# A chain of attention, mixer and routed experts: the turned keys' transposes behind the values' products, two conversion parts a step sooner, free banks first in the banks' turn

## The chip, the cores and the metric

One Trainium2 chip, one of its cores. The metric is the device time of one execution in microseconds (us). The kernel before takes 421.62 us, the median of 3 runs (421.58 to 422.22). The measurement of this kernel tells changes of some 0.2% from none.

## The reference

Three stages follow one another; each takes the output of the one before. Cut to what matters:

```python
# 1 attention with a decaying state: 2 batches, 8 heads, 768 tokens, 48 wide
y[:, :, t] = einsum('bhd,bhde->bhe', r_t, state + einsum('bhd,bhe->bhde', u * k_t, v_t))
state = w * state + einsum('bhd,bhe->bhde', k_t, v_t)
# 2 token mixing, then channel mixing, x is [2, 768, 384]
u = x + (relu(x^T @ w_tok1) @ w_tok2)^T      # 768 -> 256 -> 768
x = u + relu(u @ w_ch1) @ w_ch2              # 384 -> 1536 -> 384
# 3 eight experts; a token takes the expert of its largest logit, or,
#   where its local gate is 0.5 or more, that of the token before it
out = p[e] * (relu(x @ w1[e]) @ w2[e])       # 384 -> 1024 -> 384
```

## The kernel before, in words

**Attention** goes in 12 chunks of 128 tokens, t = 0 to 11, six for each batch. The loop over t is a pipeline written out by hand: each engine's instructions stand in the order in which the loop calls its helpers, and nothing reorders them. One turn of the loop works on several chunks at once. It calls, in this order: `old(t+1)` (PE starts the tile kp, L447), `scores(t+1)` (16 PE products into two tiles at0 and at1, L406), `pre_rk(t+2)` (DVE scales the keys and queries of a chunk, tile rk, L372), `pre_ks(t+2)` (four PE transposes of rk into the tile kt, L383, and a copy by ACT to ks, L385), `conv_ahead` (ACT, L315), `masks(t+1)` (DVE, am, L418), `beta(t+1)` (PE, into kp, L455), `pre_beta(t+2)` (DVE, pp, L377), `update(t+1)` (PE adds keys times values into kp, L464), `state(t+1)` (ACT L476, or DVE L480), `values(t)` (PE products into the tile y, L431 with the old state and L436 with the masked scores), `pre_bonus2(t+1)` (ACT copies beta out of kp, L391, and makes eight pieces of bon, L394), some parts of a weight conversion, `finish(t)` (DVE adds y and bon to x, L485; ACT and POOL split x into xh, L489, and xl, L490), from t = 7 a piece of token mixing `mix2`, then `turn(t-1)` (three PE transposes of x into the tile tp, L500, copied to xT by ACT, L501) and, from t = 4, `mix1` (PE, L357 to L359).

`pre_ks` makes ks two chunks ahead: update(t+2), in the next turn of the loop, is its only reader. It is called for all chunks but the last of each batch (5 and 11); in the loop that is at t = 0, 1, 2, 4, 5, 6, 7 and 8.

**PSUM banks.** Five banks are given out in rotation: `ps_tile` takes the next number of `turn_of` = [0, 1, 2, 3, 4], by a counter `nps`. A new tile can be written once the tile that had its bank, five calls earlier, has been read. In the loop kp, at0, at1, kt, y and tp go through this rotation; the accumulators of the mixing (`acc_tile`) have banks of their own.

**Weight conversion.** The mixer's weights arrive as 64-bit words (tile raw) in 16 blocks. Each is turned into two fp32r tiles, high and low: ACT takes the magnitude (L315), DVE works on it in three parts (L323 with L324; L328; L330), and `conv_finish` casts the high half (ACT, L291) and subtracts for the low half (POOL, L292). `conv_do(n)` works off n parts; conv_finish of a block comes at the start of the next block's first part. During attention the numbers of parts a turn are in `CONV_N`; later they are entries of a list `later`.

**Channel mixing** is a list of steps (n, f), n the quarter of the tokens, f = 0 to 11 the twelfth of the hidden width. `chan_step` makes nine PE products into a tile c of the bank rotation (`ch1`, L357 to L359), splits the result (ACT hh L362, DVE hl L363), queues `ch2`, nine products into three accumulators, which is called two steps later, and takes one entry off `later`. For n = 0 the accumulators lie in banks 2, 3 and 4 of the rotation, which then runs over banks 0 and 1 alone; after the last product of n = 0 DVE adds the three accumulators to xT (L676), and the rotation runs over all five banks again. The experts' stage behind it is not touched by the change.

Of the kernel before, what the change touches and what calls it, by code (L numbers as in the profile page):

```python
# [22 lines left out]
NCH = S // 128  # L23
NT = B * NCH
# [6 lines left out]
WARM = (6, 12, 3)  # L31
T1 = 4
CONV_N = (0, 2, 2, 3, 2, 3, 2, 2, 2, 2, 1, 0)
CONV_B = (0, 1, 0, 0, 0, 1, 1, -1, 0, 0)
HI_MIN, HI_MAX = (float(x) for x in np.array([0x38100000, 0x47EFFFFF], np.int32).view(np.float32))

# [39 lines left out]
def _emit(ctx, tc, a_in, wu, u_row, wt1, wt2, wc1, wc2, wgl, wex, cst_in, cst_a, out):  # L76
# [37 lines left out]
    turn_of, nps = [0, 1, 2, 3, 4], [0]  # L114

    def ps_tile(name, shape=(128, 512), k=None):
        if k is None:
            k = turn_of[nps[0] % len(turn_of)]
            nps[0] += 1
        return psw.tile(list(shape), F32, tag=f"w{k}", name=name)  # L120
# [10 lines left out]
    def CA(name):  # L131
        a, b = CSTA[name]
        return cta[:, a:b]
# [4 lines left out]
    def load_a(t, part=None):  # L138
        if t not in a_t:
            rk = ap.tile([128, 1024], F32, tag="rk", name=f"rk{t}", bufs=4)  # L140
            v = ap.tile([128, DM], F32, tag="v", name=f"v{t}", bufs=4)
            a_t[t] = (rk, v)
        for p, (dst, c0) in enumerate(zip(a_t[t], (0, 1536))):
            if part is None or p == part:
                nc.sync.dma_start(out=dst, in_=a_in[t, :, c0:c0 + dst.shape[1]])
# [15 lines left out]
    def warm_up(n):  # L161
        for _ in range(n):
            nc.tensor.matmul(warm_ps, lhsT=warm[:, 0:128], rhs=warm[:, 0:384], start=True, stop=True)
# [103 lines left out]
    def conv_load():  # L267
        n = nload[0]
        if n >= len(conv) or (n >= 10 and not cpool_):
            return  # L270
        nload[0] += 1
        k, h = conv[n]
        src = wt1 if k == 0 else wt2 if k == 1 else None
        if src is None:
            src = (wc1, wc2)[k % 2][(k - 2) // 2]
        if n < 10:
            raw = rawp.tile([128, 768, 2], I32, tag="raw", name="raw")
        else:
            raw = cpool_[0].tile([128, 768, 2], I32, tag=f"e{n - 10}", name="raw")
        src = src.bitcast(I32)  # L280
        if k > 1 and k % 2 == 0:
            src = src.rearrange("p (c n) -> p c n", c=3)[:, :, h * 512:(h + 1) * 512]
            nc.sync.dma_start(out=raw.rearrange("p (c n) t -> p c (n t)", c=3), in_=src)
        else:
            nc.sync.dma_start(out=raw.rearrange("p n t -> p (n t)"), in_=src[:, h * 1536:(h + 1) * 1536])
        conv_raw.append(raw)
# [52 lines left out]
    def conv_ahead():  # L339
        if abs_next[0] < 8:  # L340
            conv_abs(abs_next[0])
            abs_next[0] = 8
# [9 lines left out]
    def conv_do(n=3):  # L352
        for _ in range(n):
            next(conv_work, None)
# [15 lines left out]
    def pre_rk(t):  # L370
        rk = a_t[t][0]
        nc.vector.tensor_tensor(out=rk, in0=rk, in1=PP.rearrange("p a q j -> p (a q j)"), op=ALU.mult)  # L372
# [6 lines left out]
    def pre_ks(t):  # L379
        rk = a_t[t][0]  # L380
        kt = ps_tile("kt")
        for q in range(4):
            nc.tensor.transpose(kt[:, q * 128:(q + 1) * 128], rk[:, 512 + q * 128:512 + (q + 1) * 128], CA("ident"))  # L383
        ks_t[t] = ap.tile([128, 512], F32, tag="ks", name="ks")
        nc.scalar.copy(ks_t[t], kt)  # L385
# [3 lines left out]
    def pre_bonus2(t):  # L389
        beta = ap.tile([128, 8], F32, tag="beta", name="beta")  # L390
        (nc.scalar.copy if t % NCH else nc.vector.tensor_copy)(beta, beta_t.pop(t))  # L391
        bon = ap.tile([128, 8, D], F32, tag="bon", name="bon")
        for h in range(8):
            nc.scalar.activation(out=bon[:, h], in_=heads(a_t[t][1])[:, h], func=ACTF.Copy, scale=beta[:, h:h + 1])  # L394
        bon_t[t] = bon
# [4 lines left out]
    def scores(t):  # L400
        rk = a_t[t][0]
        at_t[t] = [ps_tile("at0"), ps_tile("at1")]
        for q in range(4):
            for g in range(2):
                r0 = 64 * g
                nc.tensor.matmul(  # L406
                    at_t[t][g][:, q * 128:(q + 1) * 128],
                    lhsT=rk[r0:r0 + 64, 512 + q * 128:512 + (q + 1) * 128],
                    rhs=rk[r0:r0 + 64, q * 128:(q + 1) * 128],
                    start=True,  # L410
                    stop=True,
                )

    def masks(t):
        am_t[t] = []
        for g, at in enumerate(at_t.pop(t)):
            am = ap.tile([128, 4, 128], F32, tag=f"am{g}", name=f"am{g}")
            nc.vector.tensor_tensor(  # L418
                out=am, in0=at.rearrange("p (h j) -> p h j", h=4), in1=C("strict").unsqueeze(1).to_broadcast([128, 4, 128]), op=ALU.mult
            )  # L420
            am_t[t].append(am)
# [20 lines left out]
    def old(t):  # L442
        kp = ps_tile("kp")
        kp_t[t] = kp[:, 0:384].rearrange("p (q e) -> p q e", q=4)
        beta_t[t] = kp[:, 384:392]
        if t % NCH in range(1, NCH - 1):
            nc.tensor.matmul(kp_t[t], lhsT=CA("ident"), rhs=sts[(t - 1) % 3], start=True, stop=False)  # L447

    def beta(t):
        pp = pp_t.pop(t)  # L450
        alone = t % NCH in (0, NCH - 1)
        for q in range(4):
            for a in range(2):
                r = slice(64 * a, 64 * a + 64)
                nc.tensor.matmul(  # L455
                    beta_t[t][r, 2 * q:2 * q + 2], lhsT=pp[:, q * 128 + 64 * a:q * 128 + 64 * a + 64], rhs=uw[:, q], start=alone, stop=alone
                )
# [118 lines left out]
    for t in range(NT):  # L576
        if t + 3 < NT:
            load_a(t + 3, 0)
        if t == 0:
            conv_load()  # L580
            conv_load()
        grow = t + 1 < NT and (t + 1) % NCH < NCH - 1
        if t + 1 < NT:
            old(t + 1)
            scores(t + 1)
            if t == 0:
                warm_up(WARM[2])
        if t + 2 < NT:
            pre_rk(t + 2)
            if (t + 2) % NCH < NCH - 1:  # L590
                pre_ks(t + 2)
        conv_ahead()
        if t + 1 < NT:
            masks(t + 1)
            beta(t + 1)
        if t + 2 < NT:
            pre_beta(t + 2)
        if grow:
            update(t + 1)
            state(t + 1)  # L600
        values(t)
        if t + 1 < NT:
            pre_bonus2(t + 1)
        if t + 3 < NT:
            load_a(t + 3, 1)
        if t < NT - 1:
            conv_do(CONV_N[t])
        finish(t)
        if t == 0:
            conv_abs(0)  # L610
        if t == NT - 1:
            conv_do(CONV_N[t])
        if t >= 7:
            mix2(*m2.pop(0))
        if t == 10:
            usplit(0)
        if t >= 1:
            turn(t - 1)
            m1.append(t - 1)
            if t >= T1:  # L620
                for _ in range(2):
                    if m1:
                        mix1(m1.pop(0))
# [39 lines left out]
    def ch2(n, f, h):  # L663
        b, half = divmod(n, 2)
        ch, cl = W[f"c2{f // 4}"]
        if f == 0:
            if n == 0:
                turn_of[:] = [0, 1]
            ch_acc[n] = [acc_tile(c) if n else ps_tile("acc", (128, 384), 2 + c) for c in range(3)]
        acc = ch_acc[n]  # L670
        for c in range(3):
            o = (f % 4) * 384 + c * 128
            mm3(acc[c], ch[:, o:o + 128], cl[:, o:o + 128], *h, f == 0, f == 11)
            if f == 11:
                u = xT[b][:, c, half * 384:(half + 1) * 384]
                nc.vector.tensor_tensor(out=u, in0=u, in1=acc[c], op=ALU.add)  # L676
        if n == 0 and f == 11:
            turn_of[:] = [0, 1, 2, 3, 4]

    later = []  # L680

# [19 lines left out]

    conv_tail(CONV_B[0])
    turn(11)
    chan_step(0, 0)
    conv_tail(CONV_B[1])
    mix1(11)
    conv_tail(CONV_B[2])
    chan_step(0, 1)
    chan_step(0, 2)
    conv_tail(CONV_B[3])  # L710
    for half in range(2):
        for c in range(3):
            mix2(1, half, c, -1 if half else (2, 0, 1)[c])
            conv_tail(CONV_B[4 + 3 * half + c])
    actx.close()
# [503 lines left out]
        for _ in side:  # L1219
            pass  # L1220

    later.extend([lambda j=j: conv_do(2 - j % 2) for j in range(16)])
    later.append(conv_do)
    order = [(0, 3), (1, 0), (1, 1), (1, 2)]
    for f in range(4, 8):
        order += [(0, f), (1, f - 1)]
# [163 lines left out]
```

## Time and profile before

| what | us |
|---|---|
| median of 3 runs | 421.62 (421.58 to 422.22) |
| the profiled execution | 421.5 |
| its span, first to last instruction | 420.0 |
| PE busy (matmul) | 397.4, 95% of the span |
| DVE busy | 274.7, 65% |
| ACT busy | 192.1, 46% |
| POOL busy | 88.4, 21% |
| mean granted TensorE clock | 0.987 of full speed |

The profiled execution lies 0.12 us under the median, and 1.5 us of it lie outside the span. Of the three stages, attention with token mixing takes about the first 100 us, channel mixing and routing go to about 200 us, and the experts take the rest. PE is busy in nearly all of the span, so the profile is read by the 22.6 us in which PE is idle: in which stretch they lie, what PE waited for there, and what the engine it waited for had been doing. In timelines each row is a run of equal instructions: its start, its length, engine and line, operation, tiles, and in brackets the idle time of that engine just before it with what ended it. Start to start, equal matmuls show the pace at which PE takes them.

### The profile page before, as it was taken

What the parts mean: (1) busy time and instruction counts of PE and PEld (TensorE: products, weight loads), DVE (VectorE), ACT (ScalarE), POOL (GpSimd) and SP (SyncE); (2) the same over time, 40 slices, a digit from 0 to 9 for tenths busy, and PEclk for the clock granted to TensorE, in tenths of its full rate; (3) what the DMA queues carried; (4) which work ended last, traced back from release to release, by engine and by line L of the source; (5) the groups of instructions that cost most, each with busy time, mean ns of one, the idle gap of its engine ahead of it and who ended that gap; (6) DMA issues with size and microseconds to landing.
All of it is one profiled execution on the core that took longest, in us unless ns stands there. A gap on an engine that the chain in (4) does not pass through costs nothing. (4 is left out here: it accounts for less than half of the span.)

```text
span 420.0 us, 8633 instructions
## 1 busy us (share of the span) xinstructions
PE 397.4 (95%) x3348; PEld 378.8 (90%) x3348; DVE 274.7 (65%) x592; ACT 192.1 (46%) x459; POOL 88.4 (21%) x83
## 2 busy tenths in 40 slices
PE   7896987999999998999999999999999999999994
PEld 3685967899999998899999999999999999999994
DVE  6799877775678987447433256759777677675430
ACT  1786566484144333221312121643755665654531
POOL 2016143333122331100000002033241222122110
PEclk9999998999999999999999999999999999999998
DMA  7746462303194000010100013781789867562000
GB/s 259 276 119 224 164 214 90 132 29 108 19 368 159 2 1 0 2 56 2 56 2 1 2 57 104 290 299 28 291 283 419 268 211 247 198 197 89 20 23 14
DMA packets 18336, 55.88 MB, mean 133 GB/s; under 512 B 3921, under 2 KB 7795, under 8 KB 18290
## 3 DMA queue, kind: packets, MB, share of 16 engines
q1 hardware_dynamic: 16370, 49.96, 33.8%
q0 software_dynamic: 1920, 5.32, 4.1%
q8 instruction: 27, 0.44, 0.4%
q14 instruction: 19, 0.16, 0.1%
HBM read 52.31 MB, written 5.91 MB: 139 GB/s over the span
## 5 line engine op out<-in xcount | busy, mean ns | idle before, releaser
L362 ACT ACTIVATE hh<-c 128x384 fp32r<-128x384 f32 x48 | 23.6, 492 | 89.7 <-PE c L359 76.8
L1038 DVE TENSOR_TENSOR we<-wr,we 128x768 fp32r<-128x768 f32 x54 | 51.6, 960 | 15.0 <-ACT we L1037 15.0
L363 DVE SCALAR_TENSOR_TENSOR hl<-c,hh 128x384 fp32r<-128x384 f32 x48 | 26.5, 553 | 40.9 <-ACT hh L362 40.9
L362 ACT ACTIVATE hh<-e 128x256 fp32r<-128x256 f32 (+1 forms) x72 | 25.2, 350 | 57.7 <-PE e L359 45.1
L363 DVE SCALAR_TENSOR_TENSOR hl<-e,hh 128x256 fp32r<-128x256 f32 (+1 forms) x72 | 27.3, 379 | 35.7 <-ACT hh L362 35.6
L357 PE MATMUL acc<-hh,c 128*128 128x384 f32 x144 | 49.6, 344 | 0.0
L358 PE MATMUL acc<-hh,c 128*128 128x384 f32 x144 | 48.4, 336 | 0.2 <-POOL c L292 0.2
L359 PE MATMUL acc<-hl,c 128*128 128x384 f32 x144 | 48.2, 335 | 0.0
L1037 ACT CAST we<-wr 128x768 fp32r<-128x768 f32 x56 | 46.0, 829 | 3.0 <-DMA wr<-in_wex 3.0
L357 PE MATMUL acc<-we,hh 128*128 128x384 f32 x120 | 42.8, 357 | 0.0
L358 PE MATMUL acc<-we,hl 128*128 128x384 f32 x120 | 40.4, 337 | 0.0
L359 PE MATMUL acc<-we,hh 128*128 128x384 f32 x120 | 40.4, 336 | 0.0
L358 PE MATMUL c<-uh,c 128*128 128x384 f32 x108 | 36.3, 336 | 2.1 <-POOL c L292 2.1
L292 POOL TENSOR_TENSOR c<-f,c 128x768 fp32r<-128x768 f32 x12 | 23.0, 1915 | 65.9 <-ACT c L291 65.9
L357 PE MATMUL c<-uh,c 128*128 128x384 f32 x108 | 36.2, 336 | 0.0
L359 PE MATMUL c<-ul,c 128*128 128x384 f32 x108 | 36.1, 335 | 0.0
L358 PEld LDWEIGHTS acc<-hh,c 128*128 128x128 f32 x144 | 27.1, 188 | 0.5 <-POOL c L292 0.5
L357 PE MATMUL e<-gx,we 128*128 128x256 f32 x96 | 27.2, 284 | 0.0
L359 PEld LDWEIGHTS acc<-hl,c 128*128 128x128 f32 x144 | 27.0, 188 | 0.0
L357 PEld LDWEIGHTS acc<-hh,c 128*128 128x128 f32 x144 | 27.0, 188 | 0.0
L359 PE MATMUL e<-gx,we 128*128 128x256 f32 x96 | 27.0, 281 | 0.0
L358 PE MATMUL e<-gx,we 128*128 128x256 f32 x96 | 27.0, 281 | 0.0
(243 smaller groups left out, 977.8 us busy)
## 6 DMA issues: line engine op xcount, KB each, us to landing
wr<-in_wex SPq DMA_DIRECT2D x32, 768.0 KB
raw<-in_wc SPq DMA_DIRECT2D x12, 768.0 KB
rk<-in_a_in SPq DMA_DIRECT2D x12, 512.0 KB
raw<-in_wt SPq DMA_DIRECT2D x4, 768.0 KB
v<-in_a_in SPq DMA_DIRECT2D x12, 192.0 KB
x<-yscr ACTq DMA_DIRECT2D x12, 192.0 KB
xs<-rows SPq DMA_DIRECT2D x8, 192.0 KB
xs<-row SPq DMA_DIRECT2D x4, 192.0 KB
```

The costliest lines, as they stand in the source:

```text
L292: nc.gpsimd.tensor_tensor(out=ls, in0=f, in1=hs.bitcast(F32), op=ALU.subtract)
L357: nc.tensor.matmul(ps, lhsT=lh, rhs=rh, start=first, stop=False)
L358: nc.tensor.matmul(ps, lhsT=ll, rhs=rh, start=False, stop=False)
L359: nc.tensor.matmul(ps, lhsT=lh, rhs=rl, start=False, stop=last)
L362: nc.scalar.activation(out=hi, in_=ps, func=ACTF.Relu)
L363: nc.vector.scalar_tensor_tensor(out=lo, in0=ps, scalar=0.0, in1=hi.bitcast(F32), op0=ALU.max, op1=ALU.subtract)
L1037: nc.scalar.copy(hi[:, cs], raw[:, cs])
L1038: eng.tensor_tensor(out=lo[:, cs], in0=raw[:, cs], in1=hi[:, cs].bitcast(F32), op=ALU.subtract)
```

## The change

`pre_ks(t+2)` is called behind `values(t)` and `pre_bonus2(t+1)`, no longer right behind `pre_rk(t+2)`. The entries of `later` follow a table `CONV_C`, in which the ninth to twelfth entry are all of two parts. After the last step of n = 0 the rotation starts anew with the two banks 0 and 1, the one whose turn it was first, and then goes to 2, 3 and 4.

```diff
+CONV_C = (2, 1, 2, 1, 2, 1, 2, 1, 2, 2, 2, 2, 1, 2, 1, 1)
...
         if t + 2 < NT:
             pre_rk(t + 2)
-            if (t + 2) % NCH < NCH - 1:
-                pre_ks(t + 2)
         conv_ahead()
...
         values(t)
         if t + 1 < NT:
             pre_bonus2(t + 1)
+        if t + 2 < NT and (t + 2) % NCH < NCH - 1:
+            pre_ks(t + 2)
...
         if n == 0 and f == 11:
-            turn_of[:] = [0, 1, 2, 3, 4]
+            a = nps[0] % 2
+            turn_of[:] = [a, 1 - a, 2, 3, 4]
+            nps[0] = 0
...
-    later.extend([lambda j=j: conv_do(2 - j % 2) for j in range(16)])
-    later.append(conv_do)
+    later.extend([lambda j=j: conv_do(j) for j in CONV_C])
```

The table adds a line, so that the lines of the changed kernel have numbers one higher. On PE only the eight groups of transposes move. Here is the turn t = 4 on PE, before (rk_648 is the chunk 6, am_668 belongs to chunk 4):

```order
L406 MATMUL at_756<-rk_541 128x128
L383 MATMUL kt<-cta,rk_648 128x128 x4
L455 MATMUL kp<-uw,pp 64x2 x8
L431 MATMUL y<-st_186,rk_439 64x96 x8
L436 MATMUL y<-v_440,am_668 64x48 x2
```

and with the change, down to the transposes of x that follow:

```order
L407 MATMUL at_756<-rk_541 128x128
L456 MATMUL kp<-uw,pp 64x2 x8
L432 MATMUL y<-st_186,rk_439 64x96 x8
L437 MATMUL y<-v_440,am_668 64x48 x2
L437 MATMUL y<-v_440,am_670 64x48 x2
L384 MATMUL kt<-cta,rk_648 128x128 x4
L501 MATMUL tp<-cta,x 128x128 x3
```

The transposes of chunk 6 stood between the scores of chunk 5 and everything else of the turn; now the products of beta and y pass them. On ACT, in the same turn, before:

```order
L501 COPY xT_535<-tp 128x3x128
L385 COPY ks<-kt 128x512
L315 ACTIVATE f<-raw 128x768
L391 COPY beta<-kp 128x8
L394 ACTIVATE bon<-v_542,beta 128x48 x8
```

and with the change:

```order
L502 COPY xT_535<-tp 128x3x128
L316 ACTIVATE f<-raw 128x768
L392 COPY beta<-kp 128x8
L395 ACTIVATE bon<-v_542,beta 128x48 x8
L386 COPY ks<-kt 128x512
```

The copy to ks moved behind the eight pieces of bon. Since kt and y change places in the bank rotation, their neighbours' banks change too: the tile at1 of a turn takes the bank of y of the turn before the last, not that of a kt. In the channel mixing the casts of the last four blocks stand one step earlier on ACT; the third of them (into c_1997) before:

```order
L362 ACTIVATE hh<-c_2136 128x384
L315 ACTIVATE f<-raw 128x768
L362 ACTIVATE hh<-c_2161 128x384
L291 CAST c_1997<-f 128x768
L362 ACTIVATE hh<-c_2189 128x384
L547 CAST uh<-xT_1202 128x384 x3
```

and with the change:

```order
L363 ACTIVATE hh<-c_2113 128x384
L316 ACTIVATE f<-raw 128x768
L363 ACTIVATE hh<-c_2138 128x384
L292 CAST c_1997<-f 128x768
L363 ACTIVATE hh<-c_2166 128x384
L363 ACTIVATE hh<-c_2190 128x384
L292 CAST c_2052<-f 128x768
L548 CAST uh<-xT_1202 128x384 x3
```

Each hh belongs to one channel step. The cast into c_1997 stood one hh ahead of the casts of uh; now it stands two ahead of them, and the fourth cast, which stood behind uh, stands in front of it. The order of instructions on POOL and SP is the same in both kernels.

## Rows read from the trace of the kernel before

**Rows 1.** Windows: stretch, length, busy us of each engine (instructions), granted clock, DMA share.

```profile
20.00:40.00 20.00, 15.79 (x318) 13.47 (x317) 19.13 (x26) 16.92 (x54) 7.04 (x5) 1.00 0.44 141
...
200.00:420.00 220.00, 213.38 (x1478) 210.68 (x1477) 125.05 (x331) 96.41 (x203) 37.25 (x38) 0.99 0.43 148
```

**Rows 2.** Waits of PE: line, waited for, us in total, times, longest.

```profile
PE kt L383 <- DVE rk L372: 7.8, 4, 4.0
PE c L358 <- POOL c L292: 2.1, 2, 1.6
...
PE acc L358 <- POOL c L292: 0.2, 1, 0.2
```

**Rows 3.** Timeline of PE, turns t = 4 and 5.

```profile
39.74 0.63 PE L383 MATMUL kt<-cta,rk 128*128 128x128 f32 x4 [3.95 <-DVE rk L372]
...
44.08 0.55 PE L500 MATMUL tp<-cta,x 128*128 128x128 f32 x3
...
46.64 1.16 PE L406 MATMUL at<-rk 64*128 64x128 f32 x16
```

**Rows 4.** Timeline of DVE, turns t = 3 to 7.

```profile
37.91 0.55 DVE L485 TENSOR_TENSOR x<-y,bon 128x384 f32<-128x384 f32 x1
38.38 1.22 DVE L372 TENSOR_TENSOR rk<-rk,PP 128x1024 f32<-128x1024 f32 x1
...
47.83 1.29 DVE L418 TENSOR_TENSOR am<-at,cst 128x512 f32<-128x512 f32 x2 [1.73 <-PE at L406]
...
54.09 2.39 DVE L372 TENSOR_TENSOR rk<-rk,PP 128x1024 f32<-128x1024 f32 x1
...
63.57 1.02 DVE L363 SCALAR_TENSOR_TENSOR t1l<-acc,t1h 128x384 fp32r<-128x384 f32 x2 [2.21 <-ACT t1h L362]
64.51 1.78 DVE L372 TENSOR_TENSOR rk<-rk,PP 128x1024 f32<-128x1024 f32 x1
```

**Rows 5.** Timeline of ACT, turn t = 4.

```profile
41.75 0.92 ACT L315 ACTIVATE f<-raw 128x768 f32<-128x768 f32 x1 [0.76 <-DMA raw<-in_wt]
42.57 0.14 ACT L391 COPY beta<-kp 128x8 f32<-128x8 f32 x1
```

**Rows 6.** Timeline of PE, turns t = 6 to 8.

```profile
56.63 0.63 PE L383 MATMUL kt<-cta,rk 128*128 128x128 f32 x4 [1.28 <-DVE rk L372]
...
59.74 0.55 PE L500 MATMUL tp<-cta,x 128*128 128x128 f32 x3 [0.49 <-ACT beta L391]
...
66.44 0.63 PE L383 MATMUL kt<-cta,rk 128*128 128x128 f32 x4 [2.32 <-DVE rk L372]
...
71.20 0.44 PE L357 MATMUL acc<-t,t1h 128*128 128x384 f32 x1
...
75.56 0.65 PE L383 MATMUL kt<-cta,rk 128*128 128x128 f32 x4
...
78.81 0.44 PE L357 MATMUL acc<-t,t1h 128*128 128x384 f32 x1
```

**Rows 7.** Windows, two stretches of lower granted clock (columns as in rows 1).

```profile
40.50:44.00 3.50, 3.50 (x64) 3.50 (x60) 3.46 (x4) 2.71 (x9) 2.19 (x2) 0.51 0.56 219
...
67.80:71.30 3.50, 3.50 (x61) 3.41 (x57) 2.19 (x4) 3.47 (x14) 0.00 (x0) 0.51 0.21 63
```

**Rows 8.** Timeline of PE in the channel mixing.

```profile
161.57 0.34 PE L359 MATMUL acc<-hl,c 128*128 128x384 f32 x1
161.74 0.40 PE L357 MATMUL c<-uh,c 128*128 128x384 f32 x1
163.69 0.44 PE L358 MATMUL c<-uh,c 128*128 128x384 f32 x1 [1.55 <-POOL c L292]
...
176.43 0.34 PE L359 MATMUL acc<-hl,c 128*128 128x384 f32 x1
177.35 0.44 PE L357 MATMUL c<-ue,c 128*128 128x384 f32 x1 [0.58 <-DVE xT L676]
```

**Rows 9.** Timeline of POOL, turn t = 4.

```profile
38.40 2.88 POOL L292 TENSOR_TENSOR t<-f,t 128x768 fp32r<-128x768 f32 x1 [3.27 <-ACT t L291]
```

## The prediction

> **What bounds the kernel now.** I read the windows first. PE is busy in 213.4 of the last 220 us, and in only 15.8 of the stretch from 20 to 40 us, where DVE is busy in 19.1 of 20 [rows 1]. So the kernel is bound by PE, except in the attention turns t = 2 to 7, where DVE hands work to PE late. The list of PE's waits says which: the largest entry is kt on rk, 7.8 us in four waits, then 2.1 us on POOL's low halves, and 0.2 more of that kind [rows 2]. The timelines give the single waits: 3.95 us at t = 4 [rows 3], 1.28 at t = 6 and 2.32 at t = 7 [rows 6]; these three make 7.55 of the 7.8. The reader should see what stands behind each on PE: beta, the state's and the values' products need nothing of that rk, yet wait with kt, since an engine works in order.
>
> **The change, part by part.** The sum is made against the profiled execution, 421.5 us, 0.12 under the median of the runs.
>
> *The transposes, t = 4.* Nothing is added or removed; eight groups of four transposes and eight copies change place. Without kt in front, PE's next obstacle is the bank of y(4), which is now that of y(3), read by x. That ends at 37.91 + 0.55 = 38.46 [rows 4]. rk ends at 38.38 + 1.22 = 39.60, so kt, behind y, no longer waits. Then tp(3) takes the bank of kp(5), as it did before; its reader is the copy of beta, which ends at 42.57 + 0.14 = 42.71, since it stands on ACT behind L315, which waits for the DMA of raw [rows 5]. That end doesn't move: the copy to ks, which leaves its place ahead of L315, lay in ACT's idle time. So tp(3) starts at about 42.75, not at 44.08 [rows 3]: **-1.33**. Of the 3.95 us only a third comes back, and the wait for the DMA is what is late next.
>
> *t = 5 and 6.* The scores at 46.64 [rows 3] come 1.33 sooner. DVE waited 1.73 us for them; its rk ended 1.73 before 47.83, at 46.10, and the scores' new time, 46.50, is still behind that, so DVE gains the full 1.33 [rows 4]. From there it works without a gap to the rk that ends at 54.09 + 2.39 = 56.48, now 55.15. On PE the scores of chunk 7 ended at 56.63 - 1.28 = 55.35, now 54.02. From kt to tp there are 59.74 - 0.49 - 56.63 = 2.62 us of work [rows 6]. With kt last of it, kt runs at about 56.1, behind rk's end at 55.15. So the wait of 1.28 goes. The 0.49 us behind it were for a copy of beta that stood on ACT behind the copy to ks; ks now comes after it. Both together: **-1.77**, and tp(5) starts at 56.64.
>
> *t = 7.* Everything is now 3.10 sooner: t1l and the rk that follows it on DVE [rows 4] end at 64.51 + 1.78 - 3.10 = 63.19. The scores ended at 66.44 - 2.32 = 64.12, now 61.02. Ahead of kt now come beta, update and y. At t = 8, where PE doesn't wait, kt, beta, update and y take 78.81 - 75.56 = 3.25 us [rows 6]; 0.6 of it is kt, so kt is reached at 63.7, half a us behind rk. **-2.32**.
>
> *The clock.* From kt to mix2 the turn t = 7 takes 71.20 - 66.44 = 4.76 us, t = 8 takes 3.25 for the same instructions [rows 6]: 1.51 us go to a granted clock of 0.51, the 1.2 GHz level, from 67.8 to 71.3 us, and the same is seen from 40.5 to 44.0 [rows 7]. Each time PE had just stood still for 2.3 to 4 us. With the wait of t = 7 gone I take the clock to stay at 2.4 GHz there: **-1.51**. At t = 4 I count nothing for the clock, since the wait for beta's copy sets the end there.
>
> *New bank waits.* at1 now takes the bank of the y before, so half of the scores wait for x(t-1) on DVE. At t = 6 the scores begin at 52.9 and x ends at 53.62 - 1.33 + 0.55 = 52.84: just level. The trace of before shows no such wait; the nearest row is a bank wait of 0.49 [rows 6]. From below: nothing, when x is always earlier. From above: 0.49 in each of the eight turns, 3.9 us. I take one, **+0.5**, since only t = 6 stands so close; at t = 2 and 3 such waits are swallowed by the 3.95 us of t = 4. The moved copies cost nothing: ks is read only by update in the next turn, behind sixteen score products; without that cover a copy's 0.6 us would be paid. From t = 8 on DVE isn't late, so the gain stays.
>
> Attention in sum: -1.33 - 1.77 - 2.32 - 1.51 + 0.5 = **-6.4**.
>
> *Conversion.* The last four blocks are finished one channel step sooner. A step is 18 products at 0.17 us start to start [rows 8], 3.1 us. The product at 163.69 came 1.95 us after its forerunner instead of 0.17, a loss of 1.78; the block would now be there 3.1 sooner, 1.3 before it is wanted. The last block's 0.2 [rows 2] goes too. **-2.0.** What could spoil it: four steps running carry two parts each, eight instead of six, and DVE falls behind; bounds are 0 and 2.0, and I take the full one since a late part must lose over 1.3 us to matter. DVE's own hl, queued behind the parts, is read two steps later, which covers it. The third wait of this kind, the rest of the 2.1, lies ahead of the blocks that move and stays.
>
> *Banks.* At 177.35 a product waits for DVE's last addition over a bank; 177.35 - 176.43 - 0.17 = 0.75 is lost [rows 8]. With banks 0 and 1 first it has a free one. **-0.75**; below that nothing, above nothing more.
>
> After this PE is the bound to the end, and the loads follow its pace. 421.5 - 6.4 - 2.0 - 0.75 = **412.3 us**. Its own range is 411.0 (no new waits, the fourth kt wait of 0.25 and further small ones gone) to 413.3 (two more waits of 0.49).
>
> **The rivals.**
>
> *The clock stays low.* At t = 4 two waits of about 2 us remain, with short work between, and if PE's pauses still pull the clock down there or at t = 7, the 1.51 us come once more: 413.8. For it: both low stretches follow pauses [rows 3, 6 and 7]. Against it: at t = 7 no pause of a size is left. Beside this stands the Trainium skill, "TensorE: Matmul & The Clock Gate", Part 4: PE-mode transpose, which says that transposes don't count as PE being busy as other matmuls do; by it kt wouldn't help to keep the clock up, and the time would be this rival's. No row here shows transposes alone.
>
> *POOL gets ahead of rk.* At t = 4 rk began at 38.38, and POOL's subtraction, which took 2.88 us, at 38.40 [rows 4, 9]. Had POOL been first, rk would take as at 54.09, 2.39 instead of 1.22, and all of DVE would be 1.17 later: 413.5. The Trainium skill, "SBUF — State Buffer", SBUF: two separate sides, has this as a lock on a port pair that DVE and POOL share, held for a whole instruction by whoever comes first; the 2.39 against 1.22 agrees.
>
> *The wait only changes its name.* If x is late at t = 6 and 7, at1 waits where kt did, and 1.28 + 2.32 = 3.6 us stay: 415.9. For it: DVE is nearly full from 20 to 40 us. Against: x stands ahead of rk on DVE, so the new wait ends 1.2 us before the old one would.
>
> *The two later edits give nothing*, should DVE's backlog hold up the blocks and another wait stand behind the bank's: 412.3 + 2.75 = 415.1.
>
> *Slower.* The bank of at1 closes a ring: y on PE, x on DVE, scores on PE, masks on DVE. Before, scores ran beside x. If x ends last in every turn, each of the eight turns grows by up to 0.49, and the kt waits are all handed on to at1; nothing of the 6.4 is left, and 421.5 + 3.9 - 2.75 = 422.7. It decides once half the scores take longer than the rk of 1.22 us that DVE works on meanwhile; all the scores take 1.16 [rows 3], so it is unlikely.
>
> *No effect.* DVE sets the pace so fully that every wait ends when it did, whatever PE does in between: 421.5. Against it: DVE itself waits for PE's scores, 1.73 us [rows 4].
>
> **How the numbers follow.** Chances: forecast 0.55, clock 0.14, POOL first 0.08, wait renamed 0.10, later edits nothing 0.06, slower 0.04, unchanged 0.03. The range from 410.0 to 415.3 holds the first three and the fifth, with 1 us below the forecast's own range for a second clock stretch gone; it leaves out 0.17. A measurement of this kernel tells 0.2%, 0.84 us, from no change: faster 0.93, same 0.03, slower 0.04.
>
> **What would show it.** Right: no wait of kt on rk over 0.5 us; at t = 4 a wait of y for x and one of tp for beta, some 2 us each; a clock near 1.00 from 60 to 80 us; the first product of channel mixing some 6.4 us sooner; of the waits on POOL's low halves only the one near 100 us; none of L357 on L676. Wrong: at or y waiting over 1 us at t = 6 and 7, low clock at t = 7, or a low half still awaited at the last blocks.

## The result

The changed kernel takes 412.23 us, the median of 4 runs (411.33 to 412.77), against 421.92 (421.58 to 422.63) for the kernel before on the same chip. The ratio is 0.9766, with a 95% interval of 0.9743 to 0.9789: 9.7 us faster, where 9.2 (412.3 us) was forecast. The profiled execution took 412.36 us, its span 410.7; before it was 420.0, so the traces differ by 9.3.

**The profile after.** First PE's list of waits (line and what it waited for, us in total, times, longest). Line numbers are one higher than before; the rows left out stand in both kernels:

```profile
PE y L432 <- DVE x L486: 2.0, 1, 2.0
...
PE c L359 <- POOL c L293: 0.6, 1, 0.6
PE tp L501 <- ACT beta L392: 0.4, 1, 0.4
PE at L407 <- DVE x L486: 0.3, 1, 0.3
```

Of the entries of [rows 2], kt on rk is gone with all its 7.8 us, the 2.1 us on POOL have become the one wait of 0.6 that was said to stay, and the 0.2 is gone; no wait on DVE's last addition (now L677) is left. New are y on x, 2.0, and at on x, 0.3. The 0.4 of tp on beta is not the old 0.49 of t = 6 but a wait at t = 8. The forecast had also named a wait of tp for beta at t = 4, of some 2 us: this trace has none.

The timeline of PE shows where the time came from. The turn t = 4, answering to [rows 3]:

```profile
35.51 0.63 PE L456 MATMUL kp<-uw,pp 128*64 128x2 f32 x16
38.13 1.55 PE L432 MATMUL y<-st,rk 128*64 128x96 f32 x16 [1.98 <-DVE x L486]
39.46 1.89 PE L437 MATMUL y<-v,am 128*64 128x48 f32 x32
41.29 1.12 PE L384 MATMUL kt<-cta,rk 128*128 128x128 f32 x4
42.20 0.85 PE L501 MATMUL tp<-cta,x 128*128 128x128 f32 x3
...
45.62 1.16 PE L407 MATMUL at<-rk 64*128 64x128 f32 x16
```

and the turns t = 6 to 8, answering to [rows 6]:

```profile
56.79 0.49 PE L501 MATMUL tp<-cta,x 128*128 128x128 f32 x3
...
63.82 0.63 PE L384 MATMUL kt<-cta,rk 128*128 128x128 f32 x4
64.20 0.42 PE L358 MATMUL acc<-t,t1h 128*128 128x384 f32 x1
...
67.46 1.64 PE L407 MATMUL at<-rk 64*128 64x128 f32 x16
...
73.84 0.55 PE L501 MATMUL tp<-cta,x 128*128 128x128 f32 x3 [0.43 <-ACT beta L392]
```

The reader should see that kt runs without a wait in both; that y, kt and tp of t = 4 take nearly double their usual time (e8 below shows it: 0.88, 1.09, 0.66 and 0.55 us); and that the scores at 67.46 take 1.64 us instead of 1.16. The clock, in two stretches (columns as in [rows 1]), after:

```profile
36.00:48.00 12.00, 10.02 (x129) 9.40 (x127) 10.83 (x14) 7.08 (x22) 5.52 (x3) 0.72 0.54 187
62.00:76.00 14.00, 13.57 (x196) 11.70 (x191) 13.87 (x20) 9.82 (x33) 4.36 (x3) 1.00 0.40 124
```

and before:

```profile
36.00:48.00 12.00, 8.26 (x101) 7.70 (x102) 10.20 (x13) 7.57 (x24) 5.54 (x3) 0.86 0.53 176
62.00:76.00 14.00, 11.68 (x142) 9.98 (x140) 9.94 (x13) 7.83 (x23) 6.53 (x4) 0.88 0.32 109
```

The granted clock at t = 7 is now 1.00 and was 0.88; at t = 4 it is 0.72 and was 0.86. The second low stretch went, the first grew longer.

**Time by stage.** Each mark is the start of a group of instructions in a PE timeline: the scores of chunk 5 and of chunk 6 (at), the first product of the channel mixing (c), the first transpose of the routing (tr), the end of the span. The experiments stand here too, so that each can be read by stage:

| kernel | to scores 5 | to scores 6 | to first c | to first tr | to the end | span |
|---|---|---|---|---|---|---|
| before | 34.6 | 12.0 | 53.3 | 79.1 | 241.0 | 420.0 |
| after | 34.4 | 11.2 | 48.2 | 75.9 | 241.0 | 410.7 |
| e1 transposes | 36.5 | 10.2 | 47.9 | 79.1 | 241.0 | 414.7 |
| e2 conversion | 34.6 | 14.1 | 54.7 | 76.7 | 243.0 | 423.2 |
| e3 banks first | 34.6 | 13.5 | 54.6 | 78.2 | 241.2 | 422.2 |
| e4 pairs only | 34.8 | 13.1 | 53.3 | 79.1 | 241.0 | 421.3 |
| e5 change again | 36.4 | 10.9 | 48.1 | 75.9 | 243.0 | 414.2 |
| e6 old pairs | 37.1 | 9.8 | 48.3 | 75.9 | 241.2 | 412.2 |
| e7 late abs | 35.0 | 9.0 | 48.7 | 75.9 | 242.9 | 411.4 |
| e8 fill t4 | 34.4 | 10.2 | 48.1 | 75.9 | 242.8 | 411.5 |
| e9 fill before | 34.6 | 10.7 | 51.8 | 79.1 | 242.9 | 419.1 |
| e10 ks ahead | 36.6 | 13.7 | 49.7 | 75.9 | 242.9 | 418.8 |
| e11 fill, late abs | 34.4 | 8.4 | 49.6 | 75.9 | 240.9 | 409.3 |

Of the 9.3 us between the two traces, 0.2 lie before the scores of chunk 5, 0.8 at t = 4, 5.05 from there to the first c, 3.2 in the channel mixing, and none behind it. The experiments ran on two chips, e1 to e4 on one and e5 to e11 on the other, on which the kernel before takes 423.5 to 424.3 us in the median and its single executions differ by up to 6 us (421.2 to 427.1), so times there are told with intervals, of 0.3 to 0.4% to either side and not the 0.2% given at the start, and the small effects are read from the stages. The channel mixing serves best for that: from the first c to tr it takes 79.08 to 79.14 us in the four traces without the two later edits (before, e1, e4, e9) and 75.89 to 75.92 in the seven with both.

### The profile page after: what moved, and what is told of

Its sections match the earlier page's. It is cut to its first block, busy times and chain, and to the rows that moved or that the text cites. A ratio compares the mean times of both kernels' runs of the same rounds, so it can differ in the third digit from the quotient of the medians.

```text
span 410.7 us, 8643 instructions
## 1 busy us (share of the span) xinstructions
PE 396.5 (97%) x3348; PEld 379.5 (92%) x3348; DVE 274.4 (67%) x592; ACT 192.1 (47%) x459; POOL 87.3 (21%) x83
## 5 line engine op out<-in xcount | busy, mean ns | idle before, releaser
L358 PE MATMUL acc<-hh,c 128*128 128x384 f32 x144 | 49.6, 344 | 0.0
L359 PE MATMUL acc<-hh,c 128*128 128x384 f32 x144 | 48.3, 336 | 0.0
L360 PE MATMUL acc<-hl,c 128*128 128x384 f32 x144 | 48.2, 335 | 0.0
```

Of the source, the lines that this page charges most:

```text
L358: nc.tensor.matmul(ps, lhsT=lh, rhs=rh, start=first, stop=False)
L359: nc.tensor.matmul(ps, lhsT=ll, rhs=rh, start=False, stop=False)
L360: nc.tensor.matmul(ps, lhsT=lh, rhs=rl, start=False, stop=last)
```

## The experiments

**The three parts, each alone.** The kernel before with one part of the change.

e1, the transposes:

```diff
             pre_rk(t + 2)
-            if (t + 2) % NCH < NCH - 1:
-                pre_ks(t + 2)
...
-            pre_bonus2(t + 1)
+            pre_bonus2(t + 1); (pre_ks(t + 2) if t + 2 < NT and (t + 2) % NCH < NCH - 1 else None)
```

> Only the transposes (and the copies to ks) moved. Theory (each part acts where it stands, the parts add up): the part of the gain up to the first product of the channel mixing, 99.91 - 93.84 = 6.1 us in the two traces, so about 415.6 against 421.7; the waits of L358 on POOL near 160 us and of L357 on L676 near 170 us stand as before. Rival (part of the later gains is a consequence of the earlier start): more than 7 us. Rival (PSUM banks): see the run in which only the banks change places.

Measured: 416.43 us, ratio 0.983 (0.9792 to 0.9869), 7.1 us faster. Its waits, from the list of PE:

```profile
PE c L358 <- POOL c L292: 2.1, 2, 1.6
PE y L431 <- DVE x L485: 2.0, 1, 2.0
...
PE c L357 <- DVE xT L676: 0.6, 1, 0.6
```

The kt waits are gone, the later two stand untouched, and the channel mixing takes 79.1 us as before. So the parts act where they stand. The time, by its interval 5.5 to 8.8 us faster, holds the theory's 6.1 and the rival's 7 alike; the untouched channel mixing decides against the rival.

e2, the conversion's table, and e3, the banks' turn:

```diff
-    later.extend([lambda j=j: conv_do(2 - j % 2) for j in range(16)])
-    later.append(conv_do)
+    later.extend([lambda j=j: conv_do(j) for j in CONV_C])
```

> Only the table of conversion parts. Theory: 1.8 + 0.3 us of waits on POOL's low halves at the last blocks go, start to start, and some 0.1 us after each for a restart: about -2.2, 419.5. The kt waits of the attention stay at 7.8 us. Rival (DVE falls behind in the four steps of two parts and holds up something else): under 1 us of gain, with a wait of PE on hl or hh that before does not have.

```diff
-            turn_of[:] = [0, 1, 2, 3, 4]
+            a = nps[0] % 2; turn_of[:] = [a, 1 - a, 2, 3, 4]; nps[0] = 0
```

> Only the order in which the five banks are taken after the last step of n = 0. Theory: the wait of L357 on L676 goes, 0.75 us and some 0.1 for the restart: about -0.85, 420.85. Rival (another tile inherits the wait a few products later): within 0.2 us of before, with a wait of a later c or tr on L676.

Measured: e2 422.47 us, ratio 0.9947 (0.991 to 0.9984); e3 423.64, ratio 0.9998 (0.9963 to 1.0033). e2 is some 2.2 us faster, as expected, with 0.7 to 3.8 by its interval; e3's time alone can't be told from before. The stages are sharper than the times: from the first c to tr, before 79.11 us, e2 76.73, e3 78.24, after 75.90. So the table gives 2.38 and the banks 0.87, and the sum, 3.25, is what the whole change gives there, 3.21. Waits of e2:

```profile
PE kt L383 <- DVE rk L372: 7.8, 4, 4.0
...
PE acc L358 <- DVE hl L363: 1.0, 1, 1.0
...
PE c L358 <- POOL c L292: 0.6, 1, 0.6
```

The wait on hl looks like the rival's sign, but lies at 315 us, in the experts' stage; the last section comes back to it. In e3's trace no wait of L357 on L676 is left, and no later c or tr waits in its place.

**The pairing of the banks.** e4 keeps the order of before and gives y its bank ahead of kt, as the change does:

```diff
+    y_a = {}
...
-        y = ps_tile("y", (128, DM))
+        y = y_a.pop(t) if t in y_a else ps_tile("y", (128, DM))
...
             if (t + 2) % NCH < NCH - 1:
+                y_a[t] = ps_tile("y", (128, DM))
                 pre_ks(t + 2)
```

> The order of before, but kt and y get their banks in the order of the change (y first, then kt), so that only the pairing of the banks is new. Theory (what counts is what stands behind kt on PE): kt waits for rk as before, 7 to 8 us in all, and at1 now can wait for x too: between 421.5 and 422.5. Rival (the new pairing of banks brings the gain): about 415.6, with the kt waits gone.

Measured: 423.9 us, ratio 1.0018 (0.9987 to 1.0049). The row at t = 4 is the old one:

```profile
39.91 1.09 PE L383 MATMUL kt<-cta,rk 128*128 128x128 f32 x4 [3.96 <-DVE rk L372]
```

In all kt waits 6.6 us for rk, in three waits, a little under the 7 to 8 expected. So the pairing brings nothing. e6 is the counterpart: the order of the change, with kt's bank taken where it was taken before. The two calls ahead of the loop are treated alike.

```diff
-        kt = ps_tile("kt")
+        kt = kt_t.pop(t)
...
             pre_rk(t + 2)
+            if (t + 2) % NCH < NCH - 1:
+                kt_t[t + 2] = ps_tile("kt")
```

> The change, but kt and y keep the banks of before (kt's is taken first although it is used after y). Theory (the order on PE brings the gain; the new pairing only adds waits): y(4) no longer waits 2.0 us for x(3), kt(6) waits instead some 1.3 us for rk, tp(3) still waits for the copy of beta, so t = 4 ends as with the change; the scores' waits for x at t = 6 to 8 (0.2, 0.1 and 0.5 us) go. 0 to 0.8 us faster than the change, first product of the channel mixing at 93.1 to 93.9. Rival (the new pairing is needed): over 1 us slower than the change.

> The changed kernel itself, for times and rows on the chip and in the hour of the next three. Theory: a low clock of some length at t = 4, 1.00 from 60 to 80 us, 75.9 us from the first product of the channel mixing to the first tr, 241.0 from there to the end; 6 to 10 us faster than before. Rival (the low clock at t = 7 comes back in some executions although no kt wait is left there): a clock under 0.95 from 60 to 80 us.

Measured on one chip: the change (e5) 413.68 us, ratio 0.9758 (0.972 to 0.9796); the old pairs (e6) 413.88, ratio 0.9779 (0.9744 to 0.9814). No difference can be told. My detail for t = 4 was wrong: y(4) did not start at once but waited longer, for another reader:

```profile
PE y L432 <- ACT xT L502: 2.5, 1, 2.5
```

With the old pairs y(4) has the bank of tp(2), whose copy stands on ACT behind the cast of x(3). In both pairings PE waits at that place for x(3), or for what stands behind its cast. The first c came at 95.15 in e6, later than the expected 93.1 to 93.9; some 2 us of that lie at the start of the span, as they do in e5 (95.35), and the last section says why. As for e5's rival: the clock from 60 to 80 us is 1.00 in e5 as in after.

**The end of t = 4.** e7 is e6 with the magnitude moved at t = 4:

```diff
-        conv_ahead()
+        if t != 4:
+            conv_ahead()
...
             pre_bonus2(t + 1)
+        if t == 4:
+            conv_ahead()
```

> As the run with the old pairs, and at t = 4 the magnitude (ACT L315), which waits for the DMA of raw, stands behind the copies of beta and bon. Theory (after the change the wait for that DMA sets the end of t = 4): tp(3) no longer waits, the scores of chunk 6 come 1 to 3 us sooner, DVE gains the 1.1 us that it still waits for them, and all that follows comes 1.1 us sooner than with the old pairs alone. Rival (DVE's chain alone sets t = 4 and 5): within 0.3 us of the run with the old pairs.

Measured: 414.3 us, ratio 0.9786 (0.9749 to 0.9823), the same as e6 within the intervals. By stage t = 4 shrinks from 9.8 us in e6 to 9.0, and the stage behind it grows from 48.3 to 48.7: 0.4 us remain, where 1.1 were expected. The expected sum took DVE's wait for the scores from the changed kernel, 1.10 us; but in e6 DVE waited far less for them:

```profile
48.07 1.29 DVE L419 TENSOR_TENSOR am<-at,cst 128x512 f32<-128x512 f32 x2 [0.24 <-PE at L407]
```

In e7 that wait is gone, and DVE works without a gap through t = 4 and 5. The rival was nearer.

**The clock.** e8 puts ten products of zeros into PE's pause in the changed kernel:

```diff
+        if t == 4:
+            warm_up(10, acc_tile(2))
         values(t)
```

> The change with ten products of zeros (1.7 us of PE work, into a free accumulator) in PE's pause at t = 4, ahead of y(4). Theory (the low clock follows PE's pause): granted clock 1.00 from 36 to 46 us, the scores of chunk 6 0.9 us sooner than with the change, and 0.9 us less in all, more against executions with a long low stretch; less spread between executions. Rival (the clock falls all the same, or the waits hide it): the scores of chunk 6 where they are with the change or later.

Measured: 412.89 us, ratio 0.974 (0.9702 to 0.9778), 0.8 faster than e5 beside it, inside the intervals; the spread is 3.4 us, against 4.2. The timeline of PE and its window:

```profile
36.08 1.80 PE L164 MATMUL acc<-upb 128*128 128x384 bf16 x10
38.14 0.88 PE L432 MATMUL y<-st,rk 128*64 128x96 f32 x16 [0.26 <-DVE x L486]
38.85 1.09 PE L437 MATMUL y<-v,am 128*64 128x48 f32 x32
39.87 0.66 PE L384 MATMUL kt<-cta,rk 128*128 128x128 f32 x4
42.09 0.55 PE L501 MATMUL tp<-cta,x 128*128 128x128 f32 x3 [1.57 <-ACT beta L392]
...
44.65 1.16 PE L407 MATMUL at<-rk 64*128 64x128 f32 x16
```

```profile
36.00:48.00 12.00, 10.17 (x169) 8.59 (x168) 11.79 (x16) 7.10 (x22) 5.50 (x3) 1.00 0.56 186
```

The clock stays at 2.4 GHz (1.00, with 0.72 in after), y takes 0.88 and 1.09 us instead of 1.55 and 1.89, and the scores of chunk 6 come 0.97 sooner (44.65, after 45.62; 0.9 was expected). One sees too what the low clock had covered: tp(3) now stands 1.57 us before the copy of beta, which stands on ACT behind the magnitude, which waits for the DMA of raw.

e9 does the same in the kernel before, at t = 4 and t = 7, without touching kt:

```diff
+FILL = {4: 20, 7: 11}
...
             pre_rk(t + 2)
+            if t in FILL:
+                warm_up(FILL[t], acc_tile(2))
             if (t + 2) % NCH < NCH - 1:
                 pre_ks(t + 2)
```

> The kernel before with products of zeros in PE's two long pauses for kt: 20 at t = 4 (3.5 us), 11 at t = 7 (1.9 us). The kt waits for rk shrink to the rest, 0.3 to 0.5 us each, but kt itself comes no sooner. Theory (part of the loss of before was the clock that falls in these pauses): granted clock 1.00 from 36 to 76 us; from the first score of chunk 5 to that of chunk 6 10.7 us and not 12.0 or more (the wait of tp for beta sets the end); from that of chunk 8 to that of chunk 9 10.0 and not 11.5 or more; some 2.8 us faster than before, and no less of the kt's own cost gone. Rival (the clock falls whatever PE does): 12.0 and 11.5 as before, or more.

Measured: 420.36 us, ratio 0.9905 (0.9873 to 0.9938), 3.9 us faster although kt comes no sooner. The timeline of PE, and the clock:

```profile
61.61 1.16 PE L407 MATMUL at<-rk 64*128 64x128 f32 x16
62.70 1.96 PE L164 MATMUL acc<-upb 128*128 128x384 bf16 x11
65.11 0.63 PE L384 MATMUL kt<-cta,rk 128*128 128x128 f32 x4 [0.45 <-DVE rk L373]
...
68.33 0.44 PE L358 MATMUL acc<-t,t1h 128*128 128x384 f32 x1
...
71.59 1.16 PE L407 MATMUL at<-rk 64*128 64x128 f32 x16
```

```profile
36.00:48.00 12.00, 11.23 (x157) 8.96 (x156) 11.58 (x15) 8.25 (x25) 5.52 (x3) 1.00 0.53 175
62.00:76.00 14.00, 13.55 (x227) 11.34 (x225) 11.76 (x17) 9.02 (x28) 4.97 (x4) 1.00 0.31 109
```

From kt to mix2 it is now 68.33 - 65.11 = 3.22 us, with 4.76 in [rows 6]; from score to score 10.67 at t = 4 and 9.98 at t = 7, where 10.7 and 10.0 were expected. The first c comes at 97.04, 2.87 sooner than before. The theory holds: part of the loss of before was not the wait but the low clock that followed it. It holds beyond the one trace: the mean granted clock of the whole execution is 0.991 to 0.999 in the six executions of e9 and 0.978 to 0.988 in the ten of before beside them.

**The copy to ks.** e10 takes the change and puts `pre_ks` between values and pre_bonus2:

```diff
         values(t)
-        if t + 1 < NT:
-            pre_bonus2(t + 1)
         if t + 2 < NT and (t + 2) % NCH < NCH - 1:
             pre_ks(t + 2)
+        if t + 1 < NT:
+            pre_bonus2(t + 1)
```

> The change with the transposes and the copy to ks ahead of the copies of beta and bon instead of behind them; the order on PE is the same. Theory (the copy to ks must not stand ahead of beta's copy, since tp waits for that): tp(3) and tp(5) wait for kt, the copy to ks and the copy of beta, some 1 us more each, in all 1 to 4 us slower than the change. Rival (only PE's order counts): the stages up to the channel mixing as with the change, within 0.3 us.

Measured: 419.64 us, ratio 0.987 (0.983 to 0.9909), by the two ratios to before 4.7 us slower than e5, where 1 to 4 were expected; the two intervals leave room for the upper end of that. PE's wait:

```profile
PE tp L501 <- ACT beta L392: 4.3, 5, 1.5
```

The mechanism is the expected one, five waits of tp for the copy of beta, 4.3 us against 1.1 in two waits in e5. The clock was lower too, 0.50 from 40 to 50 us against 0.84 in e5; what each of the two cost is not shown. That half of the change, on ACT, is needed.

**Both mendings of t = 4.** e11 takes the change with the products of e8 and the moved magnitude of e7 (both diffs above):

> The change with both mendings of t = 4: ten products of zeros in PE's pause, and the magnitude that waits for the DMA of raw behind beta and bon. Theory: the clock stays at 1.00, tp(3) follows kt at 40.4 us, the scores of chunk 6 come at about 43.3 (8.9 us behind those of chunk 5, against 10.2 with the products alone); DVE, whose rk ends at 45.7, then sets the pace, so that the first product of the channel mixing comes at 92.4 to 92.8: 1.1 to 1.4 us faster than the change, little more than either alone. Rival (PE's order sets the pace to the end): 2.3 us faster than the change.

Measured: 411.78 us, ratio 0.9715 (0.9681 to 0.9749), spans 409.3 and first c at 92.46, 1.38 sooner than after and inside the expected 92.4 to 92.8. The scores of chunk 6 stand at 42.83, 0.5 earlier than expected, and it doesn't help: PE waits for DVE instead.

```profile
PE at L407 <- DVE x L486: 1.6, 2, 1.3
```

It has the lowest ratio of the versions tried, but its interval overlaps those of e5 and e8.

## Why the prediction was right

*t = 4.* tp(3) came 1.88 us sooner, not 1.33. "That end doesn't move" was wrong of the copy of beta: the DMA of raw ended ACT's wait at 41.04 and not at 41.75 as in [rows 5], and the copy ended at 42.02.

```profile
41.04 0.92 ACT L316 ACTIVATE f<-raw 128x768 f32<-128x768 f32 x1 [1.92 <-DMA raw<-in_wt]
41.86 0.16 ACT L392 COPY beta<-kp 128x8 f32<-128x8 f32 x1
```

But the scores of chunk 6 came only 1.02 sooner. The step that failed is "At t = 4 I count nothing for the clock, since the wait for beta's copy sets the end there". There was no such wait: y and kt ran at the low clock and tp began at 42.20, straight behind kt. From tp to the scores it took 45.62 - 42.20 = 3.42 us, where before it was 46.64 - 44.08 = 2.56 [rows 3]; 0.86 went to the low clock, which reached past tp into the token mixing. e8 shows that it is the clock: there it takes 44.65 - 42.09 = 2.56 again. The two errors nearly cancel, 1.02 against 1.33, and that is luck. In e5, the same kernel, the wait for beta is there, with 0.84 us.

*t = 5 and 6.* tp(5) stands at 56.79, 2.95 sooner; 3.10 were forecast and 56.64. Both waits went as forecast, 1.93 us in this part against 1.77.

*t = 7.* kt starts at 63.82, where 63.7 was forecast, and waits for nothing. "Everything is now 3.10 sooner" was nearly true of PE (the scores come 3.01 sooner) and not of DVE: t1l began at 61.45, 2.12 sooner than in [rows 4]. rk behind it ended 62.39 + 1.28 = 63.67, half a us later than forecast and only 0.15 ahead of kt.

```profile
61.45 1.02 DVE L364 SCALAR_TENSOR_TENSOR t1l<-acc,t1h 128x384 fp32r<-128x384 f32 x2 [1.48 <-ACT t1h L363]
62.39 1.28 DVE L373 TENSOR_TENSOR rk<-rk,PP 128x1024 f32<-128x1024 f32 x1
```

Had rk taken the 1.78 us of before, kt would have waited some 0.35 us (an estimate from these rows); that it was shorter was not foreseen. mix2 starts at 64.20, 7.00 sooner; 6.93 were forecast. The share of 1.51 for the clock is borne out from two sides, by the 1.00 in the window after and by e9, where the same 1.5 us (4.76 to 3.22) come back though the wait remains.

*New bank waits.* at1 takes the bank of y of the turn just before (not of "the turn before the last", as it says ahead). One wait of 0.49 was taken, at t = 6; from mix2 (7.00 sooner) to the first c (6.07 sooner) 0.93 are given back. About half is the at1 wait that the forecast described, but at t = 8: 1.64 - 1.16 = 0.48 at 67.46, with 0.19 at t = 6. The other, 0.43 of tp for beta at 73.84, is no wait of this kind: beta's copy stood again behind the magnitude, for which ACT had waited 2.93 us on the DMA of raw. So the term was mis-sized by half, and "From t = 8 on DVE isn't late, so the gain stays" was wrong: at t = 8 PE waited for both.

*Conversion and banks.* 2.0 and 0.75 were forecast; e2 and e3 give 2.38 and 0.87. About 0.1 for each of the three waits removed is the restart: the first product behind a wait takes 0.44 us and not 0.34, and its follower starts 0.28 behind it and not 0.17. The rest is the last block, taken as 0.2, which cost 0.50 - 0.17 = 0.33 from start to start:

```profile
171.45 0.34 PE L357 MATMUL acc<-hh,c 128*128 128x384 f32 x1
171.95 0.45 PE L358 MATMUL acc<-hh,c 128*128 128x384 f32 x1 [0.17 <-POOL c L292]
172.24 0.34 PE L359 MATMUL acc<-hl,c 128*128 128x384 f32 x1
```

The feared backlog of DVE held up no block: the list of waits has none on POOL's low halves there, in e2 as in after.

*Sum.* -6.07 - 3.21 = -9.3 between the traces, -9.15 was the sum of the terms. The order on PE and the waits that it removes were read rightly. That the sum is met within 0.15 us is in part luck: the single terms miss by 0.1 to 0.4 us, in both directions.

Of the rivals, the low clock was half there: at t = 4 it stayed and lengthened, but cost 0.86 and not 1.51, since up to 42.02 tp would have had to wait for beta's copy anyway; at t = 7 it went. No run shows transposes by themselves, so the rule cited with it stays open. POOL did not get ahead of rk at t = 4: rk started at 37.99, POOL at 38.02. At t = 6 it did, as before:

```profile
53.07 2.58 DVE L373 TENSOR_TENSOR rk<-rk,PP 128x1024 f32<-128x1024 f32 x1
```

```profile
52.74 1.82 POOL L293 TENSOR_TENSOR t<-f,t 128x768 fp32r<-128x768 f32 x1 [6.18 <-DVE f L331]
```

POOL ends at 54.56 and rk 1.09 us later, about the 1.22 us that an rk takes by itself [rows 4]. The Trainium skill, "SBUF — State Buffer", SBUF: two separate sides, says that whoever comes first holds the shared ports for its whole instruction; this row agrees. So do three more rk that began while POOL worked: before 56.48 against 55.40 and 66.29 against 65.21, after 63.67 against 62.59, each 1.08 us behind POOL's end. The renamed wait came to 0.3 us on the list and not 3.6. The two later edits gave 3.2 us. Of the ring that would have made it slower, a wait of size for x at the scores is seen only in e11, 1.3 us.

## What to carry to other kernels

Look not at the engine's wait alone but at what stands behind it in order: four transposes that nobody needed for half a turn held up other products for 7.8 us, and with their consumer's copy left ahead of beta's on ACT the kernel was 4.7 us slower (e10). A pause on PE costs twice, once as a wait and once by the clock that may fall behind it, so the clock row belongs into the sum (1.5 us of 3.8 at t = 7); a term is not nothing because another wait covers it in the old trace. Effects of a microsecond that runs with a spread of 6 can't show are still told apart by the marks of the stages, where a stage takes the same time in every trace of one version.

## What the runs showed of the hardware

The low stretches of the clock differ between executions of one program. Up to the first c, e2 and e3 are the kernel before, instruction for instruction; yet in e2 the clock is 0.57 from 36 to 48 us and 0.76 from 62 to 76, where before it is 0.86 and 0.88:

```profile
36.00:48.00 12.00, 8.25 (x80) 7.86 (x81) 10.12 (x12) 7.57 (x24) 5.53 (x3) 0.57 0.51 178
62.00:76.00 14.00, 11.68 (x125) 10.51 (x125) 8.50 (x13) 9.60 (x30) 3.38 (x3) 0.76 0.32 112
```

and the first c comes at 103.43 us in place of 99.91. Against the 10.67 us of e9 at t = 4, the low clock cost before 1.35 and e2 3.45. The start of the span is such a place too. PE's first scores wait 0.9 to 2.3 us for rk, and in e1, e5 and e6 the clock is 0.57 from 8 to 16 us and all that follows comes some 2 us later; in the other ten traces it is 1.00. The same kernel, after and then e5:

```profile
8.00:16.00 8.00, 6.60 (x95) 4.91 (x97) 7.31 (x14) 3.17 (x11) 0.00 (x0) 1.00 1.02 396
8.00:16.00 8.00, 7.41 (x61) 5.38 (x62) 6.42 (x12) 2.27 (x9) 0.00 (x0) 0.57 1.03 407
```

Nor does a pause always bring the clock down: in e7 PE waited 2.5 us at t = 4 and the clock stayed at 1.00, in after it waited 1.98 and the clock fell; at the start e8 waited 2.34 and stayed at 1.00, e5 waited 1.89 and fell. That the low stretches need the pauses is shown by e9, where both were filled and the clock stayed up; e8's one trace points the same way. What decides in the single execution stays open.

The experts' stage has two lengths, 241.0 and 242.9 us from tr to the end, in no relation to the versions: the same changed kernel took 240.96 in after and 242.96 in e5. All six traces with the longer one (e2, e5, e7 to e10) have a wait of PE for hl of 0.9 to 1.0 us in it, at 315 us in e2, behind a split on ACT that starts late; none with the shorter one has it. What held the split up was not found. These two, the clock and this, make the difference between after and e5: of 3.5 us of span, 2.0 lie at the start, 2.0 in the experts' stage and -0.5 between them. Whether they make most of it between other executions of one kernel was not tried.
